# Part two without idle transposes, raw first keys, the exponential of the logits behind two copies, and keys turned first in one pair

## The chip, the cores and the metric

The kernel runs on one core of a Trainium2 chip. The metric is the device time of one execution in microseconds (us): the median of the runs shown, and beside it one profiled execution, from which every row below comes. The engines are TensorE (PE; its weight loads are listed apart as PEld), VectorE (DVE), ScalarE (ACT), GpSimd (POOL) and SyncE (SP). Each works through its own instructions in order. In this kernel SyncE issues nearly all transfers.

## The reference

Attention with decay over 4 batches and 8 heads, 768 positions of 64 features, feeds a soft mixture of 8 experts with 4 slots each. With `lam` per head, in blocks of 64 positions:

```
intra = (q_b @ k_b.T * Dmask) @ v_b                 # Dmask[i, j] = lam ** (i - j) for i >= j
inter = (q_b * lam ** (pos + 1)) @ kv_state
out_b = intra + inter
kv_state = lam ** block * kv_state + (k_b * lam ** (block - 1 - pos)).T @ v_b
...
x = out as 3072 rows of 512                         # rows: batch and position; columns: heads
logits = x @ phi                                    # 3072 x 32
d = exp(logits - max over rows), divided by its column sums + 1e-9
slot_input = d.T @ x                                # 32 x 512, four slots for each expert
slot_out = relu(slot_input[e] @ w1[e]) @ w2[e]      # 512 -> 1024 -> 512, for each expert e
c = exp(logits - max over slots), divided by its row sums + 1e-9
result = c @ slot_out                               # 3072 x 512, float32
```

## The kernel before

**Tiling.** The positions are cut into 24 tiles of 128 (six for each batch), and the attention runs over 12 pairs of tiles, `u` = 0 to 11 (lines 497 to 575). In pair `u` the tiles are `a = 2u` and `b = 2u + 1`; `c = 2u + 2` is the first of the next pair. Heads go in two halves, `hh` = 0 and 1, and four places `hp`. Products and turned copies land in eight PSUM banks with fixed names (`tr`, `dp`, `xa`, `xb`, `sc0`, `sc1`, `kv`, `gl`). A bank is taken again only when the last reader of its old content is through.

**One pair.** `natural` turns the result `xt` of the pair before into rows, into the banks `tr` and `dp`, from which ScalarE makes two copies `x`. `carry` adds the products of keys and values to the state `st`, `turn_k` turns the keys of `b` and `c` into `xa` and `xb` and copies them to `kn` (one half on VectorE times a power of lam, one half raw on ScalarE). `scores(a)` fills `sc0` and `sc1`, `scores(b)` fills `tr` and `dp`; `masked` multiplies on VectorE; `recall` multiplies queries, decayed on POOL by `decay_q` (`qs`), with the state; `attend` multiplies scores with values; `gathered` multiplies `kn` with values, one half of which POOL has decayed in `decay_v` (`vd`). At the end of an odd pair `logits` (line 376) makes the logits of four tiles: a generator that is taken forward step by step with `next(ask)`. Its first step takes the maximum on VectorE and, before the change, the exponential `e` on ScalarE; the next ones make `alpha`, a copy `L`, and the running sum. Even pairs turn `e` through `weights` (a transpose into `gl`) and add the slots' sums.

**Order.** Every engine's instructions stand in the order in which the Python code calls them (class `InOrder`); no scheduler moves them. All waits come from the tiles that are read and written. Profile lines of these calls therefore all name line 49, the helper that records them, and are told apart by tile names.

**Transfers.** SyncE issues the loads of pair `u + 2` (queries, keys, values, 256 KB each) in `feed(u)`, between them the first-layer weights (`slab`, 512 KB), then the second-layer weights (`w2t` of 256 KB, 20 `w2p` of 512 KB), and last 24 output transfers `y` of 256 KB. Up to eight are in flight; an issue also waits for its buffer.

**Experts.** `first` is the first layer. `second` (line 704) runs the second layer in quads of four matmuls, each with 256 output columns: 16 quads for the left half of the output columns (part one, bank `kv`), then 16 for the right half (part two, bank `xa`). Part two has extra work between its quads, by number, in a table `fill`: `spread(0)` and `last_C` first, `put(i, 0)` at quads 3, 5 and 7, which multiplies the left half with the weights `c`, copies it and sends it, 12 transfers in all. After part two come a copy `so`, `spread(1)` and `put(0..2, 1)`: the right half, 12 more transfers. Ahead of quads 9 to 15 stands

```
def still():
    nonlocal top
    top = bank("xb")
    idle(5)                # five transposes of the identity; nobody reads them
```

Of the kernel before, what the change touches and what calls it, by code (L numbers as in the profile page):

```python
# [8 lines left out]
F32 = mybir.dt.float32  # L9
F32R = mybir.dt.float32r  # L10
AF = mybir.ActivationFunctionType
ALU = mybir.AluOpType
AX = mybir.AxisListType

P = 128
B, H, S, DH = 4, 8, 768, 64
NB = S // P
T = B * NB
HP = H // 2
# [11 lines left out]

AT_SPREAD = 1
AT_PUTS = (3, 5, 7)
AT_IDLE = 9
AHEAD = 30
PACE = 29

# [17 lines left out]
def decay_attn_soft_moe(  # L55
# [13 lines left out]
    pe, dve, act, pool, sp = (InOrder(tc, x) for x in (nc.tensor, nc.vector, nc.scalar, nc.gpsimd, nc.sync))  # L69
# [4 lines left out]
    work = ctx.enter_context(tc.tile_pool(name="work", bufs=1))  # L74
# [4 lines left out]
    def bank(tag):  # L79
        return ps.tile([P, 512], F32, tag=tag, name=tag)  # L80
# [5 lines left out]
    IN = {}  # L86
# [75 lines left out]
    for hh in range(2):  # L162
        for hp in range(HP):
            x = hh * HP + hp
            dve.tensor_tensor_scan(
                out=mask[:, hh, hp, :],
# [22 lines left out]
    kpow = mask.rearrange("p a b i -> p (a b) i")[:, :, P - 1:P]  # L189
    CN = const.tile([P, T, SL], F32, name="CN")  # L190
    acc = const.tile([P, D], F32, name="acc")
    lsum = const.tile([P, 1], F32, name="lsum")
# [50 lines left out]
                k = slice(DH * r, DH * r + DH)  # L243
                pe.transpose(dst[r][:, i * DH:(i + 1) * DH], x[k], ident[k, k])

    def turn_k(ts, tags):

        ts = [t for t in ts if has_state(t)]
        if not ts:
            return  # L250
        tk = [bank(tag) for tag in tags]
        turn(tk, [IN[t, 1][:, hp * P:(hp + 1) * P] for t in ts for hp in range(HP)])
        n = len(ts)
        kn = [work.tile([P, 2, HP, DH], F32, tag="kn", name="kn", bufs=2) for _ in range(2)]
        tk = [x[:, 0:n * HP * DH].rearrange("p (i h c) -> p i h c", i=n, h=HP) for x in tk]
        dve.tensor_tensor(
            out=kn[0][:, 0:n],
            in0=tk[0],
            in1=kpow[:, 0:HP].rearrange("p (o h) x -> p o h x", o=1).broadcast_to([P, n, HP, DH]),
            op=ALU.mult,  # L260
        )
        act.copy(out=kn[1][:, 0:n], in_=tk[1])
        for i, t in enumerate(ts):
            KN[t] = kn[0][:, i], kn[1][:, i]

    def decay_v(ts):
        ts = [t for t in ts if has_state(t)]
        if not ts:
            return
        vd = work.tile([P, 2, HP, DH], F32, tag="vd", name="vd")  # L270
        for i, t in enumerate(ts):
            v_ = IN[t, 2].rearrange("p (h c) -> p h c", h=H)
            pool.tensor_tensor(
                out=vd[:, i],
                in0=v_[:, HP:H],
                in1=kpow[:, HP:H].broadcast_to([P, HP, DH]),
                op=ALU.mult,
            )
            VD[t] = v_[:, 0:HP], vd[:, i]
# [7 lines left out]
    def recall(t, opens):  # L287

        qs, st = QS.pop(t), ST[t - 1]
        for hp in range(HP):  # L290
            for hh in range(2):
                r = slice(64 * hh, 64 * hh + 64)
                pe.matmul(
                    out=place(t, hh, hp),
                    lhsT=st[r, hp, :],
                    rhs=qs[r, hp, :],
                    start=(opens and hp < 2),
                    stop=True,
                    skip_group_check=True,
                )  # L300
# [62 lines left out]
    def natural(ts, tags, copies):  # L363
        tr = [bank(tag) for tag in tags]
        turn(tr, [XT[t][:, hp, :] for t in ts for hp in range(HP)])
        x = keep.tile([P, 2, D], F32, tag="x", name="x", bufs=2)
        y = x.rearrange("p i (g r c) -> p r (i g) c", r=2, c=DH)
        for r in range(2):
            copies[r](out=y[:, r], in_=tr[r].rearrange("p (g c) -> p g c", c=DH))
        for i, t in enumerate(ts):  # L370
            X[t] = x[:, i]
# [4 lines left out]
    def logits(g):  # L376
        pl = bank("gl")
        for hp in range(HP):
            for c in range(4):
                pe.matmul(  # L380
                    out=pl[SL * c:SL * c + SL, 0:P],
                    lhsT=phi_sb[:, hp, :],
                    rhs=XT[4 * g + c][:, hp, :],
                    start=(hp == 0),
                    stop=(hp == HP - 1),
                )
        pl = pl[:, 0:P]
        mx = small.tile([P, 1], F32, tag="mx", name="mx")
        dve.tensor_reduce(out=mx, in_=pl, axis=AX.X, op=ALU.max)
        new = small.tile([P, 1], F32, tag="nm", name="nm")  # L390
        old = run.get("m")
        if g == 0:
            dve.tensor_scalar(out=new, in0=mx, scalar1=-1.0, scalar2=None, op0=ALU.mult)
            act.activation(out=e, in_=pl, func=AF.Exp, bias=new, scale=1.0, accum_out=lsum)
        else:
            dve.scalar_tensor_tensor(out=new, in0=mx, scalar=-1.0, in1=old, op0=ALU.mult, op1=ALU.min)
            rs = small.tile([P, 1], F32, tag="rs", name="rs")
            act.activation(out=e, in_=pl, func=AF.Exp, bias=new, scale=1.0, accum_out=rs)
        run["m"] = new
        yield  # L400
        if g > 0:
            alpha = small.tile([P, 1], F32, tag="alpha", name="alpha")
            act.activation(out=alpha, in_=old, func=AF.Exp, bias=new, scale=-1.0)
            run["alpha"] = alpha
        yield
        act.copy(out=L, in_=pl)
        yield
        if g > 0:
            dve.scalar_tensor_tensor(out=lsum, in0=lsum, scalar=alpha, in1=rs, op0=ALU.mult, op1=ALU.add)
        yield  # L410
# [84 lines left out]
    ask = sm = late_sums = iter(())  # L495
    kvs = [None]
    for u in range(NU):
        a, b, c = 2 * u, 2 * u + 1, 2 * u + 2
        opens, last = a % NB == 0, u == NU - 1
        feed(u)  # L500
        if u == NU - 2:
            for _ in range(NLOAD - 6):
                load_one(*ld1)
        if last:
            for tag, n in (("kn", 2), ("vd", 1)):
                for _ in range(n):
                    load_one(work, tag, n)

        if u > 0:
            natural((a - 2, a - 1), ("tr", "dp"), (act.copy, act.copy))  # L510
            carry(a, kvs[0][:, 1])
            decay_state(a)
            turn_k((b, c), ("xa", "xb"))
        scores(a, ("sc0", "sc1"))
        masked(a, 0)
        masked(a, 1)
        if u == 0:
            decay_v((0,))
            decay_q(1)
            turn_k((0,), ("xa", "xb"))  # L520
            scores(b, ("tr", "dp"))
        xb = [bank("xa"), bank("xb")]
        XB[a], XB[b] = (xb, 0), (xb, 2 * P)
        if u == 0:
            kv = gathered((0,))
            carry(0, kv[:, 0])
            decay_state(0)
            masked(b, 0)
            masked(b, 1)
            turn_k((b, c), ("sc0", "sc1"))  # L530
            decay_v((b, c))
            decay_q(c)
            recall(b, True)
        else:
            scores(b, ("tr", "dp"))
            masked(b, 0)
            masked(b, 1)
            if not opens:
                recall(a, True)
            recall(b, opens)  # L540
            next(ask, None)
            next(ask, None)
            next(late_sums, None)
            decay_v((b, c))
            if u == 1:
                place_phi()
            decay_q(c)
            if u % 2 == 0:
                sm = slot_softmax(u // 2 - 1, weights("gl"))
                next(sm)  # L550
            decay_q(c + 1)
        xt = keep.tile([P, 2, HP, P], F32, tag="xt", name="xt", bufs=2)

        def states():
            kvs[0] = gathered((b, c))
            carry(b, kvs[0][:, 0])
            decay_state(b)

        attend((a, b), xt, states if u % 2 == 0 else None)
        next(sm, None)  # L560
        if u == 0:
            constants()
        if u % 2 == 1 and not last:
            states()
        if u == 0:
            decay_q(c + 1)
        next(sm, None)
        if u % 2 == 1:
            ask = logits(u // 2)
            next(ask)  # L570
            if not last:
                next(ask)
        elif u > 0:
            late_sums = slots(u // 2 - 1)
            next(late_sums)
# [13 lines left out]
    def idle(n):  # L589

        for _ in range(n):
            pe.transpose(top[:, 0:P], ident, ident)
# [185 lines left out]
    fill = {AT_SPREAD: lambda: spread(0), AT_SPREAD + 1: last_C}  # L778
    for i in range(3):
        fill[AT_PUTS[i]] = lambda i=i: put(i, 0)  # L780

    def still():
        nonlocal top
        top = bank("xb")
        idle(5)

    for n in range(AT_IDLE, 16):
        fill[n] = still
    second(1, po1, fill)
    act.copy(out=so[:, HD:D], in_=po1[:, 0:HD])  # L790
    spread(1)
# [59 lines left out]
```

## Time and profile before

| What | Value |
|---|---|
| Runs shown | 161.5, 162.74 and 279.86 us; median 162.74 |
| Profiled execution | 161.27 us; span of its instructions 159.5 us |
| Busy in the span | PE 147.2 us (92%), PEld 109.4, DVE 80.6, ACT 50.3, POOL 51.3 |
| Bytes moved | 59.18 MB, 371 GB/s over the span |
| Transfers on SyncE's queue | 30544 packets, 58.80 MB |
| Mean granted clock of TensorE | 0.982 |

Busy time of an engine counts its instructions without register, branch, semaphore and DMA-issuing ones. Matmuls overlap in the array and their ends are modelled, so a busy TensorE need not be one at its peak. Between the profiled execution's time and its span lie 1.8 us outside the program's own instructions. An idle stretch of an engine matters only where others wait for it.

### The profile page before, as it was taken

The numbers are of one execution on the slowest core, as the hardware profiler recorded it, in microseconds if no ns is written. First come the engines' busy times: TensorE is split into PE (matmuls) and PEld (weight loads), VectorE is DVE, ScalarE is ACT, GpSimd is POOL, SyncE is SP. The second block draws the span as 40 slices with busy tenths as digits, with TensorE's granted clock in tenths as the row PEclk, the third lists the DMA queues.
The fourth block names the chain that finished last, engine by engine and source line by source line (L and its number), as shares of the span: only waits on it lengthen the run. The fifth ranks groups of instructions, "written<-read, shape, count | busy, mean of one in ns | idle before, by whom it ended". The sixth has DMA issues, their size and how long they took to land.

```text
span 159.5 us, 6104 instructions
## 1 busy us (share of the span) xinstructions
PE 147.2 (92%) x2614; PEld 109.4 (69%) x2614; DVE 80.6 (51%) x180; ACT 50.3 (32%) x116; POOL 51.3 (32%) x74
## 2 busy tenths in 40 slices
PE   8968999999999999999999999899999999997900
PEld 8957998789879987997789878753234645553500
DVE  0975727384957394848584966363314006300720
ACT  3012334434433453334434532430101035201610
POOL 1168683572662286553562660001000000000000
PEclk9999999999999999999999999999999999999975
DMA  5999999999999999999999999999999999991496
GB/s 170 351 396 409 412 406 408 412 389 360 402 401 398 405 401 406 410 398 394 369 398 379 420 403 394 384 395 382 401 408 408 399 408 399 387 352 41 163 384 242
DMA packets 30714, 59.18 MB, mean 371 GB/s; under 512 B 2912, under 2 KB 9184, under 8 KB 30688
## 3 DMA queue, kind: packets, MB, share of 16 engines
q1 hardware_dynamic: 30544, 58.80, 96.9%
q8 instruction: 20, 0.33, 0.7%
q14 instruction: 6, 0.05, 0.1%
q10 hardware_dynamic: 144, 0.01, 0.1%
HBM read 52.50 MB, written 6.29 MB: 369 GB/s over the span
## 4 chain that ended last, share of the span: by engine, by line
PE 87%; DVE 3%; DMA 2%; ACT 2%; issue 1%; DVEq 1%
PE xa L49 24%; PE xb L49 14%; PE gl L49 12%; PE kv L49 12%; PE tr L49 11%; PE sc L49 9%; PE dp L49 5%; DMA lam_sb<-lam_x 2%; DVE mask L49 2%; DVE qpow L49 1%; DVE at L49 1%; DVEq L847 1%; ACT so L49 0%; ACT xt L49 0%; ACT o L49 0%
## 5 line engine op out<-in xcount | busy, mean ns | idle before, releaser
L49 POOL TENSOR_TENSOR qs<-ld,qpow 128x512 f32<-128x512 f32 x20 | 25.3, 1277 | 10.3 <-issue 5.3
L49 DVE TENSOR_TENSOR at<-sc,mask 128x512 f32<-128x512 f32 x24 | 15.4, 684 | 5.1 <-PE sc L49 5.1
L49 POOL TENSOR_TENSOR vd<-ld,mask 128x256 f32<-128x256 f32 x20 | 12.4, 623 | 14.8 <-DMA ld<-vN 9.7
L49 POOL TENSOR_TENSOR dec<-st,qpow 128x256 f32<-128x256 f32 x16 | 10.0, 623 | 14.5 <-DVE st L49 10.8
L49 PE MATMUL tr<-ld 64*128 64x128 f32 x96 | 14.5, 281 | 0.0
L49 PE MATMUL sc<-ld 64*128 64x128 f32 x192 | 14.3, 292 | 0.0
L49 PE MATMUL dp<-ld 64*128 64x128 f32 x96 | 13.5, 280 | 0.0
L49 PE MATMUL xa<-at,ld 128*64 128x128 f32 x192 | 13.4, 280 | 0.0
L49 PEld LDWEIGHTS sc<-ld 64*128 64x128 f32 x192 | 12.5, 200 | 0.2 <-issue 0.2
L49 ACT COPY xt<-xa 128x512 f32<-128x512 f32 x12 | 6.9, 578 | 18.1 <-PE xa L49 18.1
L49 PE MATMUL xb<-at,ld 128*64 128x128 f32 x192 | 12.6, 273 | 0.0
L49 PE MATMUL kv<-ld,kn 128*64 128x64 f32 x160 | 11.4, 222 | 1.2 <-DVE kn L49 1.2
L49 PEld LDWEIGHTS dp<-ld 64*128 64x128 f32 x96 | 11.6, 187 | 1.1 <-ACT x L49 1.1
L49 DVE TENSOR_TENSOR st<-dec,kv 128x256 f32<-128x256 f32 x16 | 6.6, 414 | 11.3 <-PE kv L49 9.8
L49 PEld LDWEIGHTS tr<-ld 64*128 64x128 f32 x96 | 12.1, 187 | 0.2 <-ACT x L49 0.2
L49 PEld LDWEIGHTS kv<-ld,kn 128*64 128x64 f32 x160 | 10.8, 138 | 1.7 <-DVE kn L49 1.7
L49 PEld LDWEIGHTS xa<-at,ld 128*64 128x64 f32 x192 | 10.2, 136 | 2.3 <-DVE at L49 1.2
L49 PE MATMUL xb<-qs,st 64*64 64x128 f32 x160 | 11.4, 277 | 0.0
L49 PE MATMUL xa<-qs,st 64*64 64x128 f32 x160 | 11.4, 276 | 0.0
L49 PE MATMUL kv<-vd,kn 128*64 128x64 f32 x160 | 11.3, 222 | 0.0
L49 PEld LDWEIGHTS tr<-ident,xt 64*128 64x128 f32 x96 | 6.9, 139 | 6.1 <-ACT xt L49 4.7
L49 PEld LDWEIGHTS kv<-vd,kn 128*64 128x64 f32 x160 | 10.8, 138 | 0.0
(154 smaller groups left out, 328.1 us busy)
## 6 DMA issues: line engine op xcount, KB each, us to landing
slab<-w_x SPq DMA_DIRECT2D x32, 512.0 KB, 6.8
w2p<-w_x SPq DMA_DIRECT2D x20, 512.0 KB, 10.2
ld<-kT SPq DMA_DIRECT2D x24, 256.0 KB, 5.4
ld<-qT SPq DMA_DIRECT2D x24, 256.0 KB, 5.2
ld<-vN SPq DMA_DIRECT2D x24, 256.0 KB, 6.1
w2t<-w_x SPq DMA_DIRECT2D x24, 256.0 KB, 5.2
y<-o SPq DMA_DIRECT2D x24, 256.0 KB, 3.8
L<-phi_x SPq DMA_DIRECT2D x1, 64.0 KB, 4.3
```

The source lines that it names most:

```text
L49: return self._tc.keep_in_program_order(f(*args, **kwargs))
L847: with tile.TileContext(nc) as tc:
```

## The change

`order` rows below list an engine's instructions one after the other, as output<-inputs with the output's shape; equal neighbours are drawn together (x8). Line 48 in the changed kernel is line 49 before.

**1. Part two of the second layer.** `still` and its entries in `fill` go. TensorE, from the last `put(i, 0)` on (`w2p` are the weights, `hz` the hidden values), before:

```order
L49 MATMUL xa<-w2p,hz 32x256 x8
L49 MATMUL xb<-ident 128x128 x5
L49 MATMUL xa<-w2p,hz 32x256 x4
L49 MATMUL xb<-ident 128x128 x5
L49 MATMUL xa<-w2p,hz 32x256 x4
```

and now, up to the first output products of the right half:

```order
L48 MATMUL xa<-w2p,hz 32x256 x36
L48 MATMUL xb<-so,sel 32x256 x4
L48 MATMUL gl<-s_2613,CN 128x256
L48 MATMUL xb<-s_2613,CN 128x256
L48 MATMUL tr<-s_2613,CN 128x256
```

The last nine quads (36 matmuls) now stand in a row; before, five transposes stood ahead of each of the last seven.

**2. First keys.** `turn_k((0,), ..., True)` copies both halves of tile 0's keys raw on ScalarE, and `decay_first` decays all values of tile 0 on POOL (one 128x512 product in place of one of 128x256). VectorE at the start, before:

```order
L49 TENSOR_TENSOR at<-sc_166,mask 128x512
L49 TENSOR_TENSOR at<-sc_167,mask 128x512
L49 TENSOR_TENSOR kn<-xa,mask 128x256
L49 COPY st<-kv 128x256
L49 TENSOR_TENSOR at<-tr,mask 128x512
```

and now:

```order
L48 TENSOR_TENSOR at<-sc_166,mask 128x512
L48 TENSOR_TENSOR at<-sc_167,mask 128x512
L48 COPY st<-kv 128x256
L48 TENSOR_TENSOR at<-tr,mask 128x512
L48 TENSOR_TENSOR at<-dp,mask 128x512
```

The product `kn` between the masked scores and the state's copy has gone from VectorE; ScalarE has one more copy, `kn<-xa 128x256`.

**3. The exponential of the logits.** `logits` has one more step: the exponential is asked for apart from the maximum, in the next pair and behind `natural`'s two copies. `alpha` comes later too. ScalarE in pair 4, before:

```order
L49 ACTIVATE e,rs<-gl,nm 128x128
L49 ACTIVATE alpha<-nm 128x1
L49 COPY x<-tr 128x8x64
L49 COPY x<-dp 128x8x64
L49 COPY kn<-xb 128x512
L49 COPY L<-gl 128x128
```

and now:

```order
L48 COPY x<-tr 128x8x64
L48 COPY x<-dp 128x8x64
L48 ACTIVATE e,rs<-gl,nm 128x128
L48 COPY kn<-xb 128x512
L48 ACTIVATE alpha<-nm 128x1
L48 COPY L<-gl 128x128
```

The exponential has moved behind the two copies of x, `alpha` behind the copy of the keys; nothing is added.

**4. Pair 1.** `turn_k` stands ahead of `natural` in pair 1 alone, on TensorE and so on ScalarE; `carry` and `decay_state` are called ahead of `natural` in all pairs, which moves nothing on VectorE or POOL. SyncE's order of transfers is as before.

```diff
@@ -243,7 +242,7 @@
-    def turn_k(ts, tags):
+    def turn_k(ts, tags, raw=False):
@@ -253,15 +252,28 @@
         tk = [x[:, 0:n * HP * DH].rearrange("p (i h c) -> p i h c", i=n, h=HP) for x in tk]
-        dve.tensor_tensor(
-            out=kn[0][:, 0:n],
-            in0=tk[0],
-            in1=kpow[:, 0:HP].rearrange("p (o h) x -> p o h x", o=1).broadcast_to([P, n, HP, DH]),
-            op=ALU.mult,
-        )
+        if raw:
+            act.copy(out=kn[0][:, 0:n], in_=tk[0])
+        else:
+            dve.tensor_tensor(
+                out=kn[0][:, 0:n],
+                in0=tk[0],
+                in1=kpow[:, 0:HP].rearrange("p (o h) x -> p o h x", o=1).broadcast_to([P, n, HP, DH]),
+                op=ALU.mult,
+            )
         act.copy(out=kn[1][:, 0:n], in_=tk[1])
         for i, t in enumerate(ts):
             KN[t] = kn[0][:, i], kn[1][:, i]
+
+    def decay_first():
+        vd = work.tile([P, 2, HP, DH], F32, tag="vd", name="vd")
+        pool.tensor_tensor(
+            out=vd.rearrange("p a h c -> p (a h) c"),
+            in0=IN[0, 2].rearrange("p (h c) -> p h c", h=H),
+            in1=kpow.broadcast_to([P, H, DH]),
+            op=ALU.mult,
+        )
+        VD[0] = vd[:, 0], vd[:, 1]
@@ -391,12 +403,13 @@
         if g == 0:
             dve.tensor_scalar(out=new, in0=mx, scalar1=-1.0, scalar2=None, op0=ALU.mult)
-            act.activation(out=e, in_=pl, func=AF.Exp, bias=new, scale=1.0, accum_out=lsum)
+            rs = lsum
         else:
             dve.scalar_tensor_tensor(out=new, in0=mx, scalar=-1.0, in1=old, op0=ALU.mult, op1=ALU.min)
             rs = small.tile([P, 1], F32, tag="rs", name="rs")
-            act.activation(out=e, in_=pl, func=AF.Exp, bias=new, scale=1.0, accum_out=rs)
         run["m"] = new
+        yield
+        act.activation(out=e, in_=pl, func=AF.Exp, bias=new, scale=1.0, accum_out=rs)
         yield
@@ -507,17 +520,22 @@
         if u > 0:
-            natural((a - 2, a - 1), ("tr", "dp"), (act.copy, act.copy))
             carry(a, kvs[0][:, 1])
             decay_state(a)
-            turn_k((b, c), ("xa", "xb"))
+            if u == 1:
+                turn_k((b, c), ("xa", "xb"))
+            natural((a - 2, a - 1), ("tr", "dp"), (act.copy, act.copy))
+            if u % 2 == 0:
+                next(ask)
+            if u > 1:
+                turn_k((b, c), ("xa", "xb"))
         scores(a, ("sc0", "sc1"))
         masked(a, 0)
         masked(a, 1)
         if u == 0:
-            decay_v((0,))
+            decay_first()
             decay_q(1)
-            turn_k((0,), ("xa", "xb"))
+            turn_k((0,), ("xa", "xb"), True)
             scores(b, ("tr", "dp"))
@@ -540,6 +558,7 @@
             next(ask, None)
             next(ask, None)
+            next(ask, None)
             next(late_sums, None)
@@ -568,7 +587,7 @@
             next(ask)
-            if not last:
+            if last:
                 next(ask)
@@ -778,14 +797,6 @@
-    def still():
-        nonlocal top
-        top = bank("xb")
-        idle(5)
-
-    for n in range(AT_IDLE, 16):
-        fill[n] = still
     second(1, po1, fill)
```

## Rows read from the trace of the kernel before

**Rows 1.** The page, share of the span in the chain of waits

```profile
PE 87%; DVE 3%; DMA 2%; ACT 2%; issue 1%; DVEq 1%
```

**Rows 2.** Stretches: length, busy time by engine, granted clock, DMA share, GB/s

```profile
40.00:72.00 32.00, 32.00 (x682) 27.57 (x682) 21.11 (x46) 12.88 (x32) 17.14 (x22) 1.00 1.03 402
...
104.00:136.00 32.00, 31.94 (x442) 14.40 (x444) 10.57 (x29) 6.55 (x16) 0.77 (x2) 1.00 1.05 400
...
142.00:145.10 3.10, 3.10 (x38) 1.63 (x35) 0.00 (x0) 0.00 (x0) 0.00 (x0) 1.00 0.60 210
145.10:149.50 4.40, 3.14 (x49) 1.85 (x43) 1.23 (x2) 1.82 (x4) 0.00 (x0) 1.00 0.00 0
149.50:158.50 9.00, 1.93 (x22) 1.09 (x16) 2.64 (x5) 2.15 (x4) 0.00 (x0) 0.73 0.99 350
```

**Rows 3.** Timeline of SyncE, four issues: start, us, instruction, transfer

```profile
126.47 0.89 SPq L49 DMA_DIRECT2D w2p<-w_x  x1
...
140.74 0.42 SPq L49 DMA_DIRECT2D y<-o  x1
...
148.89 0.37 SPq L49 DMA_DIRECT2D y<-o  x1
...
155.21 0.56 SPq L49 DMA_DIRECT2D y<-o  x1
```

**Rows 4.** Issue to landing (last figure, us): the four, then a load issued at 81.22

```profile
w2p<-w_x SPq DMA_DIRECT2D x1, 512.0 KB, 10.4
...
y<-o SPq DMA_DIRECT2D x1, 256.0 KB, 4.3
...
y<-o SPq DMA_DIRECT2D x1, 256.0 KB, 2.2
...
y<-o SPq DMA_DIRECT2D x1, 256.0 KB, 3.3
...
ld<-qT SPq DMA_DIRECT2D x1, 256.0 KB, 4.4
```

**Rows 5.** Chain of waits, second layer: start, us, what; the pair below stands seven times

```profile
120.94 6.95 PE kv L49 x128
...
136.58 0.70 PE xb L49 x5
137.28 0.57 PE xa L49 x8
```

**Rows 6.** Start of the kernel: timeline of POOL, ACT, DVE; last row the chain

```profile
6.36 0.65 POOL L49 TENSOR_TENSOR vd<-ld,mask 128x256 f32<-128x256 f32 x1 [5.03 <-DVE mask L49]
7.99 1.27 POOL L49 TENSOR_TENSOR qs<-ld,qpow 128x512 f32<-128x512 f32 x1 [0.99 <-DVE qpow L49]
...
7.27 0.37 ACT L49 COPY kn<-xb 128x256 f32<-128x256 f32 x1 [4.63 <-PE xb L49]
...
7.84 1.26 DVE L49 TENSOR_TENSOR at<-sc,mask 128x512 f32<-128x512 f32 x2
...
9.48 0.76 PE kv L49 x15
```

**Rows 7.** Chain of waits, scores of second tile: pair 3 (first two), pair 4

```profile
33.23 0.11 PE tr L49
...
34.13 0.25 PE xa L49
...
40.77 0.22 PE tr L49 x2
...
42.14 0.25 PE xa L49
...
43.17 0.37 PE gl L49 x2
```

**Rows 8.** Timeline of ScalarE, pair 4: start, us, instruction, idle before

```profile
39.33 0.37 ACT L49 ACTIVATE e<-gl,nm 128x128 f32<-128x128 f32 x1 [1.96 <-PE dp L49]
...
40.34 0.59 ACT L49 COPY x<-dp 128x512 f32<-128x512 f32 x1
```

More of the change, by code (lines that the diff above doesn't have):

```diff
@@ L33 @@
 AT_PUTS = (3, 5, 7)
-AT_IDLE = 9
 AHEAD = 30
```

## The prediction

> **What bounds the kernel now.** I read the page first. TensorE takes 87% of the chain of waits [rows 1]: whoever stops there calls the kernel TensorE-bound and credits each microsecond saved on TensorE to the end. The table of stretches says more [rows 2]: the DMA share stands at 1.03 to 1.05 in the middle of the loop over pairs and in the expert stage, at 400 to 402 GB/s, is still 0.60 in 142.0 to 145.1 us, is 0.00 from 145.1 to 149.5, and is 0.99 until 158.5. Two resources are full at once, and the only hole in the transfers after the start is the one in front of the second half of the output.
>
> The third view is the issue of single transfers and their time to landing [rows 3, 4]. All go through SyncE's one queue. Into an empty queue the first transfer of the second output half lands 2.2 us after its issue at 148.89. A load of the loop issued at a moment when few were in flight still took 4.4, twice that. The last pair of second-layer weights, issued at 126.47, took 10.4 and landed at 136.9; the last transfer of the first output half, issued at 140.74, took 4.3 and landed at 145.04. Between these landings lie 12 transfers of 256 KB: (145.04 - 136.87) / 12 = 0.68 us each, back to back. The second half lands from 148.89 + 2.2 = 151.1 to 155.21 + 3.3 = 158.5, 7.4 us for 11 steps, 0.67 each. So there is a **floor of transfers**: bytes that no instruction of the change moves or removes keep the queue full until 145.04, whatever TensorE does, and 12 more transfers of 0.68 must follow.
>
> **Part by part.**
>
> *The idle transposes.* The chain shows part two of the second layer with seven groups of five transposes at 0.70 us, each followed by a quad at 0.57 [rows 5]. From 136.58 that is 7 x 1.27 = 8.9 us, to 145.5. Without them seven quads follow one another as in part one, where 16 quads take 6.95 us, 0.434 each: 7 x 0.434 = 3.0 us. TensorE is through 5.9 us earlier, at 139.6. Were the quads to keep 0.57, it would be 4.9. This is on the path: the copy of `so`, `spread(1)`, `put(0, 1)` and the first output copy take the 3.4 us from 145.5 to 148.89 and hang on the last quad. The first transfer of the second half would be issued at 148.89 - 5.9 = 143.0. Are the weights there? The last two quads need the landing of 136.9; they would start at 136.58 + 5 x 0.434 = 138.75, so 1.9 us are spare.
>
> *Keys of tile 0 copied raw.* VectorE leaves out `kn`, behind which the state products start at 9.48 [rows 6]. ScalarE now copies both halves, 7.27 + 2 x 0.37 = 8.0. POOL's decay of the values becomes 128x512, which I price by its `qs` of the same size at 1.27: it began at 6.36 in the trace, so ends at 7.63, and `qs`, which began at 7.99 on another wait, is not delayed. The state copy then waits for VectorE's two masked scores until 7.84 + 1.26 = 9.10 in place of 9.48 + 0.76 = 10.24, when the products were through. About 1.1 us earlier, all of it on TensorE's path.
>
> *Exponential behind the copies.* In pair 3 (odd, no exponential) the scores of the second tile take 33.23 to 34.13, 0.90 us; in pair 4 (even) 40.77 to 42.14, 1.37 [rows 7]. They need the banks that ScalarE's copies of x free; the exponential is asked for at 39.33 and the second copy ends only at 40.34 + 0.59 = 40.93 [rows 8]. With the copies first they need wait only for the transposes. 0.47 a pair, in five even pairs: 2.3 us. The bounds are 0 (the copies wait for something else) and 2.7 (should the other even pairs lose more). The exponential itself comes about 1 us later; its reader on TensorE, a transpose into `gl`, comes at 43.17 [rows 7], so nothing waits for it. `alpha` moves behind the copy of the keys and is read a pair later: nothing.
>
> *Keys of pair 1 turned first.* Both orders need a bank or tile that ScalarE's last copy of the pair before frees, so the wait stays; x's copies then come one copy of 0.59 later, or the keys' one earlier. Between a loss and a gain of 0.6 I take 0.
>
> SyncE's queue keeps its order; no transfer is added, and one early reload into a buffer of `kn` waits for ScalarE too, behind eight others in flight: 0.
>
> **The sum.** TensorE alone would be 5.9 + 1.1 + 2.3 = 9.3 us earlier. The transfers do not allow it. With the first output half landed at 145.04 and the second issued from 143.0 or earlier, the second follows without a hole: 145.04 + 12 x 0.68 = 153.2, and 1.0 us from the last landing to the end of the span as now (158.5 to 159.5) makes **154.2**. To be in time, the first issue must come by 145.04 + 0.68 - 2.2 = 143.5; the transposes' removal alone gives 143.0, so the other parts buy slack, not time. Gain 5.3 us. The profiled execution took 161.27 with 159.5 in the span: 154.2 + 1.8 = 156.0. The runs of before lie 0.2 and 1.5 us above it (the 279.86 left aside), so I say **156.2**.
>
> [...] In this trace the loads run at 400 to 402 GB/s [rows 2] and a store of 256 KB in 0.68 us, 385 GB/s. [...]
>
> **Rivals.**
>
> *The transfers come forward too.* Buffers are freed by TensorE's scores, and SyncE waits for those; a faster loop might fill the queue earlier. Then all 9.3 us count: 161.3 - 9.3 = 152.0, or anything up to 155. Against it: a share over 1 throughout, and twice the empty queue's landing time even at the lowest. 0.10.
>
> *TensorE comes after the floor.* If the loop gives nothing and the quads stay at 0.57, the first issue is at 144.0, 0.5 late: 156.5. [...] Together 0.12.
>
> *The transposes only filled a wait for weights.* Then nothing is gained, 161 to 162. It needs the last weights at 141 or later; they landed at 136.9. 0.04.
>
> [...] 0.03.
>
> The forecast has the remaining 0.71, between 155.2 and 157.4.
>
> **How the numbers follow.** The range reaches from 153.2 (faster stores, part of the first rival) to 158.6 (half clock in part two). A change of 2% is what a measurement of this kernel can tell from none: 159.5 against the median. Forecast, first and second rival lie under it; some of the second and all of the third do not. Faster 0.89, same 0.08, slower 0.03.
>
> **What would show it.** Right: quads 9 to 15 in about 3 us; scores of the even pairs at 0.90; and yet the last weights still landing near 136.9, the first output half near 145, and no hole in the transfers before the second. TensorE's lead of more than 5 us at the last quad should be larger than the gain in the span. Wrong: last weights landing 2 us or more earlier (first rival), or a hole in the transfers and a granted clock below 1.00 ahead of the last put (second).

## The result, and the profile after

The changed kernel takes 155.57 us in the median (155.03 to 156.4, 4 runs), beside 163.18 for the kernel before: a ratio of 0.957, with a 95% interval from 0.947 to 0.967. Ratios here and below compare the means of the undisturbed runs, without the run of 279.86 us of the kernel before that its median counts, so they are not quotients of the medians. Run again beside the experiments it gave 155.12, 0.961 [0.958, 0.964]. The profiled execution took 156.03 us with a span of 154.3.

In the page the share of TensorE in the chain of waits falls from 87% [rows 1] to 83%, and transfers rise from 2% to 4%; that step at the start of the kernel is taken up below.

```profile
PE 83%; DMA 4%; SPq 3%; ACT 2%; issue 1%; DVEq 1%; POOL 0%
```

The stretches (columns as in [rows 2]), from the middle of the loop to the first stores of the second output half:

```profile
40.00:72.00 32.00, 32.00 (x697) 27.94 (x696) 21.51 (x47) 13.76 (x35) 17.37 (x22) 1.00 1.04 406
104.00:136.00 32.00, 31.94 (x444) 14.30 (x440) 11.04 (x28) 6.87 (x15) 0.77 (x2) 1.00 1.05 399
...
142.00:145.10 3.10, 2.42 (x26) 1.57 (x26) 2.86 (x5) 2.48 (x5) 0.00 (x0) 1.00 1.04 363
145.10:149.50 4.40, 0.00 (x0) 0.00 (x0) 0.27 (x1) 0.01 (x1) 0.00 (x0) 0.56 1.09 384
```

The hole has closed: in 145.1 to 149.5, where the DMA share was 0.00 before [rows 2], it is 1.09, and TensorE has nothing left to do. Of these stretches its granted clock is below 1.00 only in that one (0.56), when no work hangs on it.

The four issues of [rows 3] on SyncE, now (last pair of weights; last store of the first output half; first and last of the second):

```profile
126.01 0.72 SPq L48 DMA_DIRECT2D w2p<-w_x  x1
...
139.22 0.78 SPq L48 DMA_DIRECT2D y<-o  x1
...
141.88 0.37 SPq L48 DMA_DIRECT2D y<-o  x1
...
148.24 0.57 SPq L48 DMA_DIRECT2D y<-o  x1
```

and their time from issue to landing, as in [rows 4]:

```profile
w2p<-w_x SPq DMA_DIRECT2D x1, 512.0 KB, 10.2
...
y<-o SPq DMA_DIRECT2D x1, 256.0 KB, 5.9
y<-o SPq DMA_DIRECT2D x1, 256.0 KB, 3.9
y<-o SPq DMA_DIRECT2D x1, 256.0 KB, 5.1
```

The weights land at 136.2 (136.9 before) and the first half at 139.22 + 5.9 = 145.1 (145.04 before). The second half is issued 7.0 us earlier, but its first store takes 3.9 us in place of 2.2: it stands in the queue. It lands at 145.8, the next slot of 0.68 after 145.1, and the last at 153.3.

The chain of waits of the second layer (start, us, what; as in [rows 5]):

```profile
119.78 6.95 PE kv L48 x128
...
134.41 4.07 PE xa L48 x72
...
138.50 0.38 ACT so L48
```

Nine quads in one row take 4.07 us, 0.45 each. The copy of `so` behind the last quad starts at 138.50; in the profile of before it started at 145.51.

### The profile page after: what moved, and what is told of

Its sections match the earlier page's. It is cut to its first block, busy times and chain, and to the rows that moved or that the text cites. A ratio compares the mean times of both kernels' runs of the same rounds, so it can differ in the third digit from the quotient of the medians.

```text
span 154.3 us, 6028 instructions
## 1 busy us (share of the span) xinstructions
PE 139.9 (91%) x2579; PEld 105.6 (68%) x2579; DVE 80.4 (52%) x179; ACT 50.4 (33%) x117; POOL 51.8 (34%) x74
## 4 chain that ended last, share of the span: by engine, by line
PE 83%; DMA 4%; SPq 3%; ACT 2%; issue 1%; DVEq 1%; POOL 0%
PE xa L48 22%; PE gl L48 13%; PE xb L48 12%; PE kv L48 11%; PE tr L48 11%; PE sc L48 9%; PE dp L48 5%; DMA ld<-vN 4%; SPq L48 3%; DVEq L858 1%; ACT so L48 0%; POOL vd L48 0%; ACT xt L48 0%; ACT o L48 0%; ACT e L48 0%
## 5 line engine op out<-in xcount | busy, mean ns | idle before, releaser
L48 POOL TENSOR_TENSOR vd<-ld,mask 128x256 f32<-128x256 f32 (+1 forms) x20 | 12.9, 645 | 21.5 <-DMA ld<-vN 16.4
L48 PE MATMUL tr<-ld 64*128 64x128 f32 x96 | 13.4, 277 | 0.3 <-DMA ld<-kT 0.3
L48 ACT COPY x<-tr 128x512 f32<-128x512 f32 x12 | 7.0, 586 | 14.7 <-PE dp L48 11.2
L48 PEld LDWEIGHTS xa<-at,ld 128*64 128x64 f32 x192 | 10.2, 136 | 2.3 <-issue 1.4
L48 PE MATMUL kv<-ld,kn 128*64 128x64 f32 x152 | 10.9, 222 | 0.0
L48 PEld LDWEIGHTS xb<-at,ld 128*64 128x64 f32 x192 | 10.7, 137 | 0.0
## 6 DMA issues: line engine op xcount, KB each, us to landing
w2p<-w_x SPq DMA_DIRECT2D x20, 512.0 KB, 10.2
```

The lines of the kernel that those rows point to most:

```text
L48: return self._tc.keep_in_program_order(f(*args, **kwargs))
```

## The experiments

Two theories stand against each other. **Transfers**: the first output half lands at a time that TensorE does not set, and the second needs 12 slots after it. **TensorE**: the end follows the first issue of the second half, so each microsecond of TensorE counts. All kernels below were timed in five rounds beside the kernel before. A landing is the start of an issue plus its time to landing.

**The changed kernel again** (no edit).

> The changed kernel once more, beside the next three on one chip. Both theories: 155.6 us, a ratio of 0.957 to the kernel before. In its profile the first output half should be landed near 145.1 and the right half should follow without a hole, with the last quad ended near 138.5.

155.12 us, ratio 0.961 [0.958, 0.964]; span 153.3. In this profile the transfers are earlier than in the first one, the last weights by 0.5 us (issued at 125.51, landed at 135.7) and the output by 0.9 (the first half landed at 138.62 + 5.6 = 144.2). TensorE is earlier too (its copy of `so` at 137.30). So two profiles of one kernel differ by 0.9 us in the floor itself, and a single one places a step of less than that only roughly.

**Ten, and thirty, matmuls ahead of the last quad.** The removed idle transposes come back at one place, in a size of choice.

```diff
+    def still():
+        nonlocal top
+        top = bank("xb")
+        idle(10)          # e_hold_30: idle(30)
+
+    fill[15] = still
     second(1, po1, fill)
```

> The changed kernel with ten transposes (about 1.4 us of TensorE) put back, all of them ahead of the last quad. Theory of transfers: the first transfer of the right half is issued at about 143.3, still ahead of 143.5, where the queue would run dry, so the time stays at 155.6 (within 0.3). Theory of TensorE (the end hangs on the last quad): 1.4 later, 157.0.

> The same with thirty transposes (about 4.2 us). Theory of transfers: the first issue comes at about 146.1, 2.6 behind the point at which the queue runs dry, so 158.2, with a hole of about 2.6 us in the transfers ahead of the right half. Theory of TensorE: 4.2 later, 159.8.

Ten: 156.04 us, 0.965 [0.962, 0.968], span 154.6. Thirty: 158.01 us, 0.980 [0.976, 0.983], span 156.8. With thirty the delay of the chain is 3.43 us:

```profile
135.12 3.59 PE xa L48 x64
138.72 3.43 PE xb L48 x30
142.14 0.61 PE xa L48 x8
142.78 0.38 ACT so L48
```

and SyncE's timeline has the last store of the first half, and the first of the second:

```profile
139.76 0.42 SPq L48 DMA_DIRECT2D y<-o  x1
...
146.15 0.37 SPq L48 DMA_DIRECT2D y<-o  x1
```

The first half takes 4.3 us to landing (144.1) and the second 2.2 (148.4), into an empty queue. The stretch shows the hole, a DMA share of 0.33:

```profile
144.00:148.40 4.40, 3.79 (x48) 2.79 (x48) 2.62 (x5) 2.52 (x6) 0.00 (x0) 1.00 0.33 115
```

By the ratios to the kernel before (161.48) thirty lose (0.9795 - 0.9609) x 161.48 = 3.0 us. The times alone do not decide: the transposes took 3.43 us and not the 4.2 expected, and with intervals of about 0.6 us on each time 3.0 cannot be told from 3.4 or from the 2.6 of the transfers. The rows do: the first issue of the second half comes 4.3 us later than in the first profile of the changed kernel (146.15 against 141.88), and 5.5 later than in the second, while the span grows by 2.5 and 3.5. Of the delay 1.8 and 2.0 us are lost in slack.

Ten, expected at 0 by the transfers and at 1.4 by TensorE, cost 0.6 to 0.9 us (ratios, medians), between the two, and the intervals of its ratio and of the changed kernel's still touch. Its profile says why it need not be 0: TensorE came out of the loop 0.7 us later there than in the first profile of the changed kernel, so the first issue stood at 143.99 and missed its slot by 1.1 us. The slack that has to be used up first is small: by the table below, 0.4 to 2.1 us in the five profiles in which transfers set the end and TensorE has its full lead.

**Fewer bytes ahead of the first output half.** The last 8 weight tiles of w2's second half are not loaded; the quads 12 to 15 use other weights in their place, so they compute something else at the same cost.

```diff
-    while late:
+    while len(late) > 8:
         load_two()
+    for q in range(4):
+        for f in (6, 7):
+            wt["w2", 1, q, f] = wt["w2", 1, q, f - 2]
```

> The changed kernel without the last four weight transfers (2 MB, some 5.1 us of the queue); quads 12 to 15 of part two multiply with weights loaded for other columns of the hidden layer in their place, so that much of the second layer is not what the reference computes. TensorE's work is the same. Theory of transfers: the left half is through before the right half is issued at about 141.9, so that now TensorE sets the end: 141.9 + 2.2 + 7.4 + 1.0 = 152.5 in the span, 154.0 in time, 1.6 faster than the changed kernel. Theory of TensorE: no change, 155.6.

154.28 us, 0.952 [0.949, 0.956]: 0.9% or 1.4 us less than the changed kernel, with the same work on TensorE. The theory of transfers expected 154.0 and that of TensorE no change (155.6), so transfers are a bound; and the end is not as early as the bytes alone would allow. SyncE's timeline of its profile (its execution took 155.98 us, the longest of the six, with part one of the second layer starting 1.7 us later than in the first profile of the changed kernel):

```profile
121.21 0.37 SPq L48 DMA_DIRECT2D w2p<-w_x  x1
...
139.47 1.15 SPq L48 DMA_DIRECT2D y<-o  x1
...
143.56 0.37 SPq L48 DMA_DIRECT2D y<-o  x1
```

The last weights land 10.2 us after their issue, at 131.4, 5 us before those of the changed kernel. The last of the first half lands at 143.8, behind other stores. The first of the second takes 2.2 us, so it found the queue nearly empty, and the stretch from its issue to its landing has a DMA share below 1:

```profile
143.70:145.70 2.00, 2.00 (x25) 1.56 (x26) 1.87 (x3) 1.40 (x3) 0.00 (x0) 1.00 0.66 231
```

With these bytes gone TensorE sets the end in this profile. The two bounds of the changed kernel lie within 1 to 2 us of each other.

**The removal of the idle transposes alone** (the kernel before, without them), in two batches of runs.

```diff
-    def still():
-        nonlocal top
-        top = bank("xb")
-        idle(5)
-
-    for n in range(AT_IDLE, 16):
-        fill[n] = still
     second(1, po1, fill)
```

> The kernel before without the idle transposes, and nothing else of the change. Theory of transfers: the first transfer of the right half is issued near 143.1, about 0.4 ahead of the point at which the queue runs dry, so the whole gain is there: 155.6 to 156.2, a ratio of 0.957 to 0.962. Theory of TensorE: about 1.1 us slower than the whole change, 156.7, since the last quad ends that much later.

> The kernel before without the idle transposes once more, beside the kernel before on one chip, since the first profile of it held 8.6 us of pauses in the landings where the others held 4.6 to 5.4. Theory of transfers: last left landing near 144.5, first issue near 143.1, and so max(144.5 + 0.68, 143.1 + 2.2) + 7.45 + 1.0 = 153.7 in the span, 155.5 in time. If the other three parts of the change are worth something here, as the first run of it says: 156.7 to 157.

157.06 us, 0.969 [0.963, 0.974], and 156.16 us, 0.966 [0.963, 0.970]. The whole change stood at 0.961. In the second profile SyncE issued

```profile
140.64 0.44 SPq L49 DMA_DIRECT2D y<-o  x1
...
143.55 0.37 SPq L49 DMA_DIRECT2D y<-o  x1
```

with 4.3 and 2.2 us to landing: the first half is in at 144.9, and the second begins at 145.8, 0.2 us after its slot. The span is 154.2. The first profile is that of the longest of its six executions (158.67 us, the others 155.74 to 158.02); its span of 156.9 has the last weights at 139.5, with more pauses between landings than the profiles taken until then (below). The times of the first batch lie on the side that the theory of TensorE expected (156.7), those of the second between the two expectations; the part on why the prediction was right takes this up.

**The other three parts alone** (the changed kernel with the idle transposes put back).

```diff
+    def still():
+        nonlocal top
+        top = bank("xb")
+        idle(5)
+
+    for n in range(9, 16):
+        fill[n] = still
     second(1, po1, fill)
```

> The whole change, but with the idle transposes kept. Here both theories let the end hang on the last quad; what is in question is what the three other parts are worth on TensorE. If waits for loads took what the first keys and the exponential gained, as in the profile of the changed kernel, about 1.2 us: 160.1 (ratio 0.993). If the prediction's terms hold, 3.4 us: 157.9 (ratio 0.979).

160.31 us, 0.990 [0.985, 0.994]: 1.7 us (1.0 to 2.4), between the two expected ratios and nearer the smaller gain. The first issue comes at 148.26 and lands after 2.2 us; there is a hole again, so TensorE sets the end, and here its gain upstream counts in full. That makes it a measure of the gain.

**The exponential alone** (the kernel before, with the step of `logits` split and asked for behind the copies of x).

```diff
         run["m"] = new
         yield
+        act.activation(out=e, in_=pl, func=AF.Exp, bias=new, scale=1.0, accum_out=rs)
+        yield
...
-            natural((a - 2, a - 1), ("tr", "dp"), (act.copy, act.copy))
             carry(a, kvs[0][:, 1])
             decay_state(a)
+            natural((a - 2, a - 1), ("tr", "dp"), (act.copy, act.copy))
+            if u % 2 == 0:
+                next(ask)
             turn_k((b, c), ("xa", "xb"))
```

> The kernel before with the exponential behind the copies alone (idle transposes kept). If the prediction's term holds, the scores of the second tile take 0.90 us in the even pairs as in the odd ones and the last quad comes 2.3 us earlier: 159.0 (ratio 0.986). If TensorE runs into the loads instead, less than 1 us: above 160.3.

160.19 us, 0.989 [0.984, 0.993], 1.8 us (1.1 to 2.6), so that the forecast's 2.3 is not excluded. Alone it is worth as much as the three parts together, so that the raw copy of the keys and the order of pair 1 come to about nothing between them, within intervals of some 0.7 us to either side.

**Pair 1 in the old order** (the changed kernel; `natural` ahead of `turn_k` in all pairs).

```diff
-            if u == 1:
-                turn_k((b, c), ("xa", "xb"))
             natural((a - 2, a - 1), ("tr", "dp"), (act.copy, act.copy))
             if u % 2 == 0:
                 next(ask)
-            if u > 1:
-                turn_k((b, c), ("xa", "xb"))
+            turn_k((b, c), ("xa", "xb"))
```

> The whole change with pair 1 in the order of the other pairs (x turned ahead of the keys). If the order of pair 1 cost what the profile of the changed kernel suggests, the scores of the second tile of pair 1 take 0.90 us in place of 1.42, and TensorE reaches the first layer up to 0.5 earlier. Theory of transfers: the time stays at 155.6. Theory of TensorE: 155.1.

155.23 us, 0.959 [0.954, 0.964], the same as the changed kernel; the 0.5 us in question is less than these times can tell. In the traces the order does cost something. Chain of waits, scores of the second tile of pair 1, in the changed kernel:

```profile
17.36 0.26 PE tr L48 x2
...
18.78 0.25 PE xa L48
```

and with the old order:

```profile
16.66 0.11 PE tr L48
...
17.55 0.25 PE xa L48
```

1.42 us against 0.89. The new order loses 0.5 us on TensorE. In the profile of the old order the transfers set the end, by 0.4 us (table below), so that the floor would hide it; the times alone do not show that.

**The kernel before again** (no edit), as a control in the third batch.

> The kernel before once more, to see where its transfers land in another execution. Theory of transfers: the last weights land at 136 to 137 and the left half at 144 to 145, as in the changed kernel, with a hole of about 4 us ahead of the right half. Rival (transfers come forward with TensorE): they land about 1 us later here than in the changed kernel's profiles.

161.82 us, 1.002 [0.998, 1.005], span 160.9. Its last weights land at 127.54 + 10.5 = 138.0, and the first half at 146.3. The theory of transfers expected 136 to 137 and 144 to 145, so this came out as the rival had it: the transfers of the kernel before land 1.2 to 2.4 us later than those of the changed kernel in its two profiles. The stretch in front of the second half is empty:

```profile
146.40:151.50 5.10, 3.84 (x54) 2.27 (x48) 1.58 (x3) 2.21 (x5) 0.00 (x0) 1.00 0.05 19
```

**Two queues for the second half** (the changed kernel; every second store issued by ScalarE).

```diff
-            sp.dma_start(out=rows[:, t:t + 5:4, half * HD:(half + 1) * HD], in_=o)
+            queue = act if half == 1 and r % 2 == 0 else sp
+            queue.dma_start(out=rows[:, t:t + 5:4, half * HD:(half + 1) * HD], in_=o)
```

> The whole change, with every other transfer of the right half issued by ScalarE on its own queue in place of SyncE's. If the 0.68 us for a store is what the engines behind both queues can do, nothing moves: 155.3 (0.67 to 0.68 from landing to landing). If it is what one queue can do, the right half lands at the loads' 0.64 or faster: 0.5 us or more earlier, 154.8 or less.

155.34 us, 0.961 [0.957, 0.965]: the same. ScalarE's first store was issued at 142.21 and took 3.5 us to landing, its last 5.0:

```profile
142.21 0.45 ACTq L48 DMA_DIRECT2D y<-o  x1
...
147.90 0.59 ACTq L48 DMA_DIRECT2D y<-o  x1
```

The first lands at 145.7, the last at 152.9: 11 steps of 0.65 us, against 0.68 from one queue. A gain of 0.5 us lies within the interval of the time, but the rows show that a second queue shortens the step by no more than 0.03 us: what limits the stores is not the one queue.

**A smaller lead of the weight loads** (the changed kernel).

```diff
-AHEAD = 30
+AHEAD = 20
```

> The whole change with one 512 KB transfer of first-layer weights fewer ahead of the loads of queries, keys and values, which so land up to 1.3 us sooner. If waits for these loads hold TensorE in the loop, the pairs run at 7.6 to 8.0 us without the stretched ones, and TensorE reaches the first layer about 1 us earlier. Theory of transfers: the end stays at 155.3, or comes later if the queue now runs dry in the loop. Theory of TensorE: about 1 us faster, 154.3.

156.43 us, 0.967 [0.964, 0.970], 1.0 us slower than the changed kernel. TensorE is not the cause, since its copy of `so` starts at 138.57 (138.50 in the changed kernel). The transfers are:

```profile
140.60 0.46 SPq L48 DMA_DIRECT2D y<-o  x1
...
141.94 0.37 SPq L48 DMA_DIRECT2D y<-o  x1
```

The first half takes 5.0 us to landing, so 145.6, and the second stands behind it for 4.4. The weights came at 137.4. What was moved in 20 to 90 us, in this kernel:

```profile
DMA packets 11277, 27.82 MB, mean 397 GB/s; under 512 B 1253, under 2 KB 1253, under 8 KB 11262
```

and in the changed one:

```profile
DMA packets 11423, 28.13 MB, mean 402 GB/s; under 512 B 1267, under 2 KB 1267, under 8 KB 11408
```

0.31 MB less: at 402 GB/s that is 0.8 us, which would be most of the loss. It is one profile against few: the changed kernel's second profile moved 28.58 MB in the same stretch, and that of fewer bytes, with the same loop and the larger lead, 27.9 (399 GB/s over 70 us). So the floor is not wholly fixed by the bytes: what is allowed to be in flight during the loop moves it, to judge by the time.

**One rule for all fourteen profiles.** The second half begins to land at the later of two times: the first half's last landing plus a slot of 0.68, or the first issue plus 2.24. Then come 7.45 us for the other 11 stores, and 1.0 to the end of the span. Worked out from the rows of each profile (us):

| kernel | last weights | first half landed | first issue | by transfers | by TensorE | end by the rule | span |
|---|---|---|---|---|---|---|---|
| before | 136.9 | 145.1 | 148.9 | 145.8 | **151.1** | 159.6 | 159.5 |
| before again | 138.1 | 146.3 | 150.3 | 147.0 | **152.6** | 161.0 | 160.9 |
| the other three parts | 136.0 | 144.2 | 148.3 | 144.8 | **150.5** | 159.0 | 158.9 |
| the exponential alone | 136.1 | 144.3 | 147.5 | 144.9 | **149.8** | 158.2 | 158.1 |
| thirty matmuls held | 135.9 | 144.1 | 146.2 | 144.8 | **148.4** | 156.8 | 156.8 |
| ten matmuls held | 136.2 | 144.4 | 144.0 | 145.1 | **146.2** | 154.7 | 154.6 |
| fewer bytes | 131.4 | 143.8 | 143.6 | 144.5 | **145.8** | 154.3 | 154.2 |
| transposes alone, second | 136.4 | 144.9 | 143.6 | 145.6 | **145.8** | 154.2 | 154.2 |
| transposes alone, first | 139.5 | 147.7 | 144.0 | **148.4** | 146.3 | 156.9 | 156.9 |
| the change | 136.2 | 145.1 | 141.9 | **145.8** | 144.1 | 154.2 | 154.3 |
| the change again | 135.7 | 144.2 | 140.7 | **144.9** | 142.9 | 153.4 | 153.3 |
| pair 1 as before | 135.4 | 143.6 | 141.7 | **144.3** | 143.9 | 152.7 | 152.8 |
| two queues | 136.5 | 144.7 | 142.2 | **145.4** | 144.5 | 153.8 | 153.9 |
| smaller lead | 137.4 | 145.6 | 141.9 | **146.3** | 144.2 | 154.8 | 154.8 |

The rule gives every span to 0.1 us. The two constants 7.45 and 1.0 are read from these same profiles, so what it shows is which of two ends binds where, and that nothing else does. With two queues two deviations cancel: the first store lands 0.3 us after the rule's 145.4, and the other 11 need 7.2 (145.7 to 152.9). The profiles of fewer bytes and of the transposes alone, first, are those of the longest of their six executions.

## Why the prediction was right, step by step

The forecast of 156.2 us (153.2 to 158.6) stands against 155.57 in the median and 156.03 in the profiled execution, for which its sum gave 156.0.

**The floor of transfers** held: span 154.2 forecast, 154.3 found. TensorE was through 7.0 us earlier at the last quad, and the span gained 5.2, with no hole in front of the second half. A lead larger than the gain is what the forecast had named as the mark of its cause. That the span agrees to 0.1 us is luck: the same kernel again had 153.3, and in the five profiles in which transfers set the end and TensorE has its full lead the first half landed anywhere from 143.6 to 145.6. The stores ran at 384 GB/s in the stretch 145.1 to 149.5.

**The range** rests at both ends on terms that no run shows: 153.2 on faster stores, where one queue gave 0.68 us for 256 KB and two gave 0.65, and 158.6 on half clock in part two, where TensorE's granted clock stayed 1.00 to 145.1 in the changed kernel. Part of the 0.12 of the second rival, and the 0.03 for a slower kernel, rest on such a clock too.

**The idle transposes** were sized right: from the start of part one to the last quad's end before took 145.51 - 120.94 = 24.6 us and takes 138.50 - 119.78 = 18.7 now, 5.9 less, as the forecast had it. With the last weights in at 136.2, TensorE's weight loads waited once for them in part two. The table of waits (who, for what: us in all, count, longest):

```profile
PEld xa L48 <- DMA w2p<-w_x: 0.2, 1, 0.2
```

**The parts upstream** were forecast too large: 3.4 us of lead at the start of part one, of which the first profile has 1.2 (119.78 against 120.94) and the second 2.4. The kernel before again started part one 1.5 us later than its first profile, so single pairs of profiles say little; timed alone the parts give 1.7. By their terms:

*The exponential*, 2.3 forecast, 1.8 measured alone. In pair 4 the mechanism is as forecast: the scores of the second tile take 0.89 us where they took 1.37 [rows 7]. Chain of waits:

```profile
41.00 0.11 PE tr L48
...
41.89 0.25 PE xa L48
```

The time from the last copy `xt` of an odd pair to the first of the next shrinks by 0.3 to 0.5 us (pair 2 from 7.77 to 7.46, pair 4 from 8.20 to 7.72). That of pair 6 stretches from 7.13 to 7.78 instead and gives part of it back.

*The first keys*, 1.1 forecast; by the second copy `xt` 0.1 in this profile and 0.7 to 0.9 in others. Two things were not foreseen. First, a load of values landed at 12.23 where it had landed at 11.18, and POOL's next decay waited for it, with TensorE behind it:

```profile
12.30 0.62 POOL L48 TENSOR_TENSOR vd<-ld,mask 128x256 f32<-128x256 f32 x1 [1.07 <-DMA ld<-vN]
```

That is the transfers' share of 4% in the chain, which leads through this load:

```profile
5.90 6.33 DMA ld<-vN
```

Second, the forecast held the masked scores at 7.84 [rows 6], but the wider product on POOL delays them. Timeline of POOL and VectorE in the changed kernel:

```profile
6.45 1.08 POOL L48 TENSOR_TENSOR vd<-ld,mask 128x512 f32<-128x512 f32 x1 [5.11 <-DVE mask L48]
...
6.59 1.22 DVE L48 TENSOR_TENSOR_SCAN qpow<-lam_sb,zero 128x128 f32<-128x128 f32 x1
...
8.36 1.26 DVE L48 TENSOR_TENSOR at<-sc,mask 128x512 f32<-128x512 f32 x2
```

VectorE's scan runs beside POOL's product and takes 1.22 us, and the masked scores behind it start at 8.36, 0.5 us later than before. POOL's `qs`, which the forecast held at 7.99, starts at 8.52 for the same reason.

*The order of pair 1*, 0 forecast, with bounds of 0.6 either way: a loss of 0.5 us, near the lower bound.

"The other parts buy slack, not time" is too strong. The transposes alone stood at 0.966 and 0.969, the whole at 0.957 and 0.961: 0.5 to 1.2%, 0.8 us by the closest pairs, at the edge of the intervals. Two things can make it. In the second profile without the other parts the first issue was needed by 143.4 and came at 143.55, so the edge ran through the scatter of runs; and the other parts move the floor, as follows.

**The transfers came forward too**, in part, as the first rival had it with a chance of 0.10. The last weights land at 136.4 to 139.5 in the four profiles with the older loop and at 135.4 to 136.5 in eight with the exponential moved (without fewer bytes and the smaller lead); the first output half at 144.9 to 147.7 and at 143.6 to 145.1. The bytes moved in 20 to 90 us go the same way. The kernel before, and the changed kernel again:

```profile
DMA packets 11320, 27.79 MB, mean 397 GB/s; under 512 B 1254, under 2 KB 1254, under 8 KB 11305
...
DMA packets 11540, 28.58 MB, mean 408 GB/s; under 512 B 1278, under 2 KB 1278, under 8 KB 11524
```

Against the 27.79 MB of the kernel before, the changed kernel moved 28.13 and 28.58 there, and fewer bytes, whose loop is the same, 27.9: 0.1 to 0.8 MB more, 0.3 to 2.0 us at 402 GB/s. The exponential alone has the last weights at 136.1 (table). So the premise that the queue stays full to the same moment "whatever TensorE does" held only to about 1 us. The DMA share over this stretch, 1.03 in the kernel before and 1.03 and 1.04 in the changed one, hid it. The size fits what the sum did not give: by its ratio the changed kernel gains 6.3 us of 161.48 where the sum had 5.3, and the whole is 0.8 us ahead of the transposes alone.

**Open.** By which wait the loop holds the transfers back is not shown. By sums over the table of SyncE's waits in 8 to 104 us, from the kernel before to the first profile of the changed one, those for TensorE fall from 25.5 to 21.7 us and those for landings rise from 16.3 to 24.2, which fits a TensorE that frees buffers earlier, but no run sets this wait alone. The landings also pause at places that no experiment set: between 12 us and the last weights, 7 intervals in the kernel before are longer than 0.65 us for each 256 KB by 0.4 to 1.2 us, 5.1 us in sum, and 5 in the changed kernel by 0.3 to 1.5, 3.8 in sum; for the first profile of the transposes alone the expectation of the second counts 8.6. In one of the changed kernel's the DMA engines go on (a share of 1.04 in 112.9 to 114.5). What sets them is open. None of the versions run is clearly below the changed kernel with all of its computation kept: pair 1 in the old order (0.959) and two queues (0.961) lie within its interval.

## What to carry to other kernels

When a chain of waits names one engine and the DMA share is full at the same time, look for the hole in the transfers: the end is the later of two times, the landing of what is queued and the first issue behind it, and an edit on the engine behind the queued transfers is worth only the width of that hole. Whether a single store found the queue empty is read from its time to landing (2.2 us here, 2.4 and more behind others). Past that point a microsecond taken off the engine there buys slack alone, and the next gain lies in bytes, in what is kept in flight, or in a faster stage upstream that lets transfers go earlier (about 1 us here). A profile is one execution: the floor itself moved by 0.9 us between two of the same kernel.

## What the runs showed of the hardware

POOL held up VectorE here: the scan of 128x128 that took 1.22 us beside the POOL product of 1.08 took 0.78 in the kernel before, beside a product of 0.65, and the scan ahead of it took 0.40 in both:

```profile
6.50 0.78 DVE L49 TENSOR_TENSOR_SCAN qpow<-lam_sb,zero 128x128 f32<-128x128 f32 x1
```

The difference of 0.44 us is that between the two products (1.08 - 0.65 = 0.43), and the scan ends 0.28 and 0.27 us behind the product: 7.81 against 7.53 now, 7.28 against 7.01 before [rows 6]. By the chain of waits or the timeline, 2.07 to 2.09 us pass from the last scan into `mask` to the first masked scores in all nine profiles with the wider product, 1.64 to 1.65 in the five without it. Why is not shown. Widening a product on POOL was not free for VectorE, although POOL itself had time.

A DMA share above 1 does not say that the DMA engines could move no more: over 20 to 90 us it was 1.03 in the kernel before, with 27.79 MB moved, and 1.03 and 1.04 in the two profiles of the changed one, with 28.13 and 28.58. And a second queue hardly shortened the stores: 0.65 us for 256 KB with two, 0.68 with one.
